# Reordering the prologue and the first steps of a 24-step recurrent scan on one Trainium2 core

## The chip, the cores and the metric

The kernel runs on one core of a Trainium2 chip. TensorE multiplies matrices, VectorE, ScalarE and GpSimd work elementwise, SyncE issues most transfers; the profile calls them PE, DVE, ACT, POOL and SP. The metric is device time in microseconds (us) of one execution, the median of several.

## The reference

For each of 4 x 8 heads a 40 x 40 state is carried over 768 time steps; the result goes through a gated feed-forward block.

```python
for t in range(S):                                   # S = 768
    y[:, :, t] = einsum('bhd,bhde->bhe', rt, state)
    Sa = einsum('bhde,bhe->bhd', state, at)
    state = state * wt[:, :, None, :] - einsum('bhd,bhe->bhde', Sa, bt)
    state = state + einsum('bhd,bhe->bhde', vt, kt)
x = y.transpose(0, 2, 1, 3).reshape(B, S, H * D)
h = maximum(x @ w_in, 0); u, v = halves of h         # 320 -> 1024
v_n = layernorm(v); v_s = einsum('ts,bsd->btd', w_spatial, v_n) + b_spatial
out = (u * v_s) @ w_out
```

## The kernel before, in words

The 768 time steps are cut into chunks of 64, and two batches (8 units of 2 heads) go together, so the first phase has 24 chunks, called steps 0 to 23. Inside a chunk the recurrence is a small triangular system; its solution lets the state jump 64 time steps at once. The second phase does the spatial product and the projection.

**What is made for a chunk before its step.** Its inputs arrive in a tile `ein` in two parts: W, the decay columns (528 columns), and O, the other operands (1536 columns). DVE runs two scans over W (`scan1`, L286, with a reciprocal L290; `scan2`, L295), giving running decay products `S` and `Et`. Then it multiplies: `at` (L312) from O and `Et`, `sl` (L318) from O and `S`. From `at` and `sl` PE makes the triangles (`lprime`, L331, 64 small products), and DVE masks them into `Lc` (`lblock`, L342). PE also makes `lka` (L392), `tok` (L444, transposes), `l21` (L461) and `h` (L422, from the tile `lin`), which ACT copies out of PSUM. ACT copies a column of `S` into the tiny tile `sc` (L304), which SP stores for a later step (`scr`, L306).

**The solve.** Four chunks' triangles are inverted together on DVE (`invert`, L350 to L367): a transpose, thirty pairs of products and additions, two more transposes into `XT0` (L365) and `X11` (L367). The first such solve stands alone in the prologue; later ones are spread through the steps. For each chunk PE and ACT then finish the inverse `xf`: `zt` (product L480, copies L489), copies of `XT0` (`b_xcopy`, L762) and `x21` (product L507, copies L516).

**A step.** `bp` (PE L538, reading the state `Mc`), its copies (ACT L548), `ff` (PE L556), copies `ffs` (ACT L564), `xx` (PE L574, needs `xf`), copies and masks (ACT L585, POOL L399), `mp` (PE L606), the new state `mn` and `Mc` (DVE L619, L620), and the output `y` (PE L630, DVE L643). There is one `bp` buffer per group of units, so the next step's `bp` waits for the DVE `y` instruction as well as for `Mc`.

**What sets the order.** In the first phase each engine runs its instructions strictly in the order in which they are written out; nothing reorders them. The prologue is straight code. From step 0 on a plan is used: `at(t, function, args)` enters a function at time t in units of steps, the plan is sorted by t, and the functions are called in that order. So a number such as 0.66 says how far through a step an item is issued, and an item that waits holds up everything behind it on its engine. While step s runs, the other work for chunk s+1 is issued (`b_...` functions), and the chunks' scans run some steps ahead: chunk 4 and 5's during step 0, 6 and 7's during step 1, 8 and 9's during step 2. The tiles `ein` of these are loaded in six pieces per chunk (`prep_piece`, L273, on SP) into two alternating buffers, a buffer being free once the chunk two earlier has made its `sl`.

Of the kernel before, what the change touches and what calls it, by code (L numbers as in the profile page):

```python
# [8 lines left out]
F32 = mybir.dt.float32  # L9
# [15 lines left out]
NU = NB * NP  # L25
GS = 4
# [185 lines left out]
def phase1(ctx, tc, early, late, vtok, win, xs, vns, uts, dscr):  # L212
# [48 lines left out]
    st = {}  # L261
# [58 lines left out]
            in1=sv[:, ns, 2:C + 2].unsqueeze(2).broadcast_to([P, k, 2, C]), op=ALU.mult,  # L320
        )

    def lprime(s):
        Et, at, sl = st["pre", s]
        pl = ps_k.tile([P, NU, HB], F32, name="bk")
        for n in range(NU):
            for blk in range(2):
                for par in range(2):
                    o = (1 - par) * 64 + blk * HB
                    cs = slice(blk * HB, (blk + 1) * HB)  # L330
                    nc.tensor.matmul(  # L331
                        pl[o:o + HB, n, :], lhsT=sl[PR[par], n, par, cs], rhs=at[PR[par], n, cs],
                        start=True, stop=True,
                    )
        st["pl", s] = pl

    def lblock(s):
        if s % GS == 0:
# [34 lines left out]
    def lin_load(s, par):  # L373
        nc.sync.dma_start(out=lin[s % 2][RR[par], :, 0:LATE], in_=late[par, s])
# [378 lines left out]
    def at(t, fn, *args):  # L753
        plan.append((t, len(plan), fn, args))
# [15 lines left out]
    for s in range(NS):  # L770
        at(s + 0.02, scn_load, s)
        for g in range(NB):
            at(s + 0.00 + 0.05 * g, c_bp, s, g)
            at(s + 0.04 + 0.05 * g, c_bp_out, s, g)
            at(s + 0.30 + 0.05 * g, c_ff, s, g)
            at(s + 0.34 + 0.05 * g, c_ff_out, s, g)
            at(s + 0.55 + 0.05 * g, c_xx, s, g)
            at(s + 0.60 + 0.05 * g, c_xx_out, s, g)
            at(s + 0.74 + 0.02 * g, c_mp, s, g)
            at(s + 0.755 + 0.02 * g, c_mp_out, s, g)  # L780
            at(s + 0.86 + 0.04 * g, c_y, s, g)
            at(s + 0.90 + 0.04 * g, c_y_out, s, g)
            at(s + 0.95 + 0.01 * g, y_store, s, g)
    for q in range(1, NS):
        b = q - 1
        for par in range(2):
            at(b + 0.11 + 0.02 * par, b_copy, q, par)
            at(b + 0.17 + 0.02 * par, b_lka_out, q, par)
            at(b + 0.72 + 0.02 * par, b_h_out, q, par)
            at(b + 0.40 + 0.03 * par, b_tok, q, par)  # L790
            at(b + 0.43 + 0.03 * par, b_tok_out, q, par)
        at(b + 0.115, b_lka, q)
        at(b + 0.52, b_l21, q)
        at(b + 0.54, b_l21_out, q)
        z = q % GS == 0
        at(b + (0.88 if z else 0.66), b_zt, q)
        at(b + (0.90 if z else 0.68), b_zt_out, q)
        at(b + 0.68, b_h, q)
        at(b + (0.975 if z else 0.50), b_xcopy, q, XC)
        at(b + (1.12 if z else 0.78), b_x21, q)  # L800
        at(b + (1.16 if z else 0.81), b_x21_out, q)
    for q in range(2, NS):
        for par in range(2):
            at(q - 2 + 0.20 + 0.14 * par, lin_load, q, par)
            at(q - 1 + 0.48 + 0.14 * par, vtok_load, q, par)

    LPO = 0.93
    PREP = {4: 0.03, 5: 0.45, 6: 1.03, 7: 1.45, 8: 2.03, 9: 2.45, 10: 3.03, 11: 3.45}
    for q in range(GS, NS):
        t = PREP.get(q, q - 8 + 0.01)  # L810
        at(t + 0.20, scan1, q)
        at(t + 0.28, scan2, q)
        at(t + 0.285, scr_store, q)
        at(t + 0.29, at_mul, q, AT_ENG)
        at(t + 0.30, sl_mul, q, SL_ENG)
        if q + 2 < NS:
            gap = 0.07 if q < 12 else 0.14
            for k in range(6):
                at(t + 0.40 + gap * k, prep_piece, q + 2, k)
        at(t + LPO, lprime, q)  # L820
        at(t + LPO + 0.05, lblock, q)
# [43 lines left out]
    with tc.manual_schedule():  # L865
# [11 lines left out]
            )  # L877
        pads(p, ein[2])
        pads(p, ein[3])
        for q in range(GS):  # L880
            for cols in (W, O):
                prep_load(q, 48 if q else 64, cols, q, qs)
        for par in range(2):
            lin_load(0, par)
            vtok_load(0, par)
# [10 lines left out]
        for q in range(2):  # L896
            for rows in RR:
# [1 line left out]
                nc.scalar.activation(  # L899
                    lin[q][rows, :, LATE:], diag.unsqueeze(1).broadcast_to([E, NU, E]), AF.Copy  # L900
                )
        for q in range(GS):
            scan1(q, q)
            scan2(q)
            at_mul(q, v)
            sl_mul(q, v)
            scr_store(q)
            lprime(q)
            if q:
                lblock(q - 1)  # L910
            if q == 0:
                b_copy(0, 0)
                b_copy(0, 1)
            if q == 1:
                b_lka(0)
                b_tok(0, 0)
                b_tok_out(0, 0)
            if q == 2:
                b_lka_out(0, 0)
                b_lka_out(0, 1)  # L920
                b_tok(0, 1)
                b_tok_out(0, 1)
                b_l21(0)
                b_l21_out(0)
        lblock(GS - 1)
        for par in range(2):
            lin_load(1, par)
            vtok_load(1, par)
        prep_load(4, 48)
        prep_load(5, 48)  # L930
        b_h(0)
        for _ in invert(0):
            pass
        b_h_out(0, 0)
# [71 lines left out]
```

## Time and profile before

| | us |
|---|---|
| median of 3 runs | 700.64 |
| lowest, highest | 698.61, 700.89 |
| the profiled execution, device time | 700.49 |
| its span in the profile | 698.8 |
| PE, DVE, ACT, POOL busy | 580.5, 445.9, 387.1, 297.7 |

The span runs from the first to the last instruction of the profile; the device time is 1.7 us longer. A timeline row gives start and busy time in us, then engine, source line, operation, output tile, input tiles, shapes and the number of instructions merged; the bracket at its end is the idle time of that engine just before and what ended it. A windows row gives for a stretch its length, the busy time of PE, PEld, DVE, ACT and POOL with instruction counts, then the granted PE clock, the busy share of the DMA engines and GB/s. A waits row gives who waited for whom, the us in total, the number of times and the longest.

### The profile page before, as it was taken

Reading aid. Unit: us, or ns where it says so; the run is one execution under the profiler, and the core shown is the slowest. Engines: PE = TensorE matmul, PEld = TensorE weight load, DVE = VectorE, ACT = ScalarE, POOL = GpSimd, SP = SyncE. Lnnn points to the kernel's source line nnn. Section 1 sums busy time; section 2 is a strip of 40 time slices with the busy share of each in tenths; the row PEclk is TensorE's granted clock in tenths of the full one; section 3 lists DMA queues with packets and bytes.
Section 4 is the critical chain, followed back from the end, with each engine's and each line's share of the span. In section 5 each row is a group of like instructions: output and inputs, shape, how many; then the busy total and the mean of one; then the engine's idle time right before and its main releaser. Section 6 shows DMA issues by size and latency. Waiting matters only on the chain. (4 is left out here: it accounts for less than half of the span.)

```text
span 698.8 us, 25621 instructions
## 1 busy us (share of the span) xinstructions
PE 580.5 (83%) x10784; PEld 528.8 (76%) x10784; DVE 445.9 (64%) x884; ACT 387.1 (55%) x856; POOL 297.7 (43%) x486
## 2 busy tenths in 40 slices
PE   1716885578777777999987999999999999999997
PEld 1615774477666667888876788788889989999997
DVE  7898779988999999968887366612128521332221
ACT  2305752356554666688867788898855442421112
POOL 5101332115434555364653434545448972462221
PEclk9965998678886986999999899999999999999999
DMA  9562877366454634766466355446345465550001
GB/s 184 97 115 50 141 146 138 74 145 135 102 131 107 142 83 122 142 152 153 118 174 197 89 146 149 123 131 166 97 139 170 132 177 162 164 180 28 29 30 57
DMA packets 106333, 87.68 MB, mean 125 GB/s; under 512 B 35497, under 2 KB 92073, under 8 KB 104297
## 3 DMA queue, kind: packets, MB, share of 16 engines
q1 hardware_dynamic: 105672, 84.31, 48.8%
q10 hardware_dynamic: 544, 1.72, 1.1%
q8 instruction: 85, 1.39, 0.9%
q14 instruction: 32, 0.25, 0.1%
HBM read 59.20 MB, written 20.50 MB: 114 GB/s over the span
## 5 line engine op out<-in xcount | busy, mean ns | idle before, releaser
L399 POOL TENSOR_SCALAR_AFFINE_SELECT Rt<-Rt 64x512 f32<-64x512 f32 (+1 forms) x144 | 86.4, 601 | 107.1 <-ACT Rt L585 73.6
L548 ACT ACTIVATE Rt<-bp 64x416 f32<-64x416 f32 x96 | 49.2, 512 | 73.3 <-PE bp L538 71.5
L538 PE MATMUL bp<-lin,Mc 40*64 40x104 f32 x768 | 52.2, 298 | 29.9 <-DVE y L643 29.3
L399 POOL TENSOR_SCALAR_AFFINE_SELECT At<-At 64x512 f32<-64x512 f32 x48 | 41.8, 871 | 77.2 <-ACT At L409 61.3
L356 DVE TENSOR_TENSOR itmp<-A 128x30 f32<-128x30 f32 (+9 forms) x180 | 72.0, 400 | 3.3
L538 PEld LDWEIGHTS bp<-lin,Mc 40*64 40x64 f32 x768 | 45.4, 164 | 33.2 <-DVE y L643 32.1
L173 PE MATMUL pg<-wsh,vh 128*128 128x384 f32 x192 | 65.2, 340 | 0.0
L174 PE MATMUL pg<-wsl,vh 128*128 128x384 f32 x192 | 65.2, 340 | 0.0
L175 PE MATMUL pg<-wsh,vl 128*128 128x384 f32 x192 | 65.1, 339 | 0.0
L360 DVE TENSOR_TENSOR A<-A,itmp 128x30 f32<-128x30 f32 (+9 forms) x180 | 59.0, 328 | 6.2
L177 DVE TENSOR_TENSOR g<-pg,bb 128x384 f32<-128x384 f32 x32 | 17.8, 556 | 65.0 <-PE pg L175 60.1
L54 POOL TENSOR_TENSOR gl<-g,gh 128x384 fp32r<-128x384 f32 x32 | 33.7, 1053 | 51.6 <-ACT gh L50 51.4
L585 ACT ACTIVATE Rt<-ch 64x416 f32<-64x416 f32 x96 | 49.2, 512 | 4.2 <-PE ch L574 1.8
L556 PE MATMUL ch<-Rt,At 128*64 128x104 f32 x768 | 46.6, 279 | 1.0 <-issue 1.0
L556 PEld LDWEIGHTS ch<-Rt,At 128*64 128x64 f32 x768 | 40.8, 154 | 5.4 <-issue 2.8
L50 ACT ACTIVATE gh<-g 128x384 fp32r<-128x384 f32 x32 | 16.6, 521 | 49.3 <-DVE g L178 49.1
L574 PE MATMUL ch<-ffs,xf 64*64 64x104 f32 x768 | 43.1, 266 | 0.0
L480 PE MATMUL bk<-XT,l 32*32 32x32 f32 x768 | 18.9, 201 | 28.4 <-DVE XT L365 26.4
L54 POOL TENSOR_TENSOR vl<-raw,vh 128x512 fp32r<-128x512 f32 x24 | 32.2, 1349 | 23.6 <-ACT vh L50 19.7
L480 PEld LDWEIGHTS bk<-XT,l 32*32 32x32 f32 x768 | 16.1, 116 | 32.8 <-issue 22.6
L708 DVE BATCH_NORM_STATS2 bs<-vr 128x6 f32<-128x512 f32 x24 | 16.6, 690 | 37.4 <-ACT vr L702 37.2
L444 PE MATMUL bk<-ident,sl 128*128 128x128 f32 x192 | 30.7, 301 | 11.7 <-ACT tk L450 7.0
(134 smaller groups left out, 1569.3 us busy)
## 6 DMA issues: line engine op xcount, KB each, us to landing
ein<-in_early SPq DMA_DIRECT2D x108, 129.0 KB
lin<-in_late SPq DMA_DIRECT2D x48, 160.0 KB
At<-at SPq DMA_DIRECT2D x48, 128.0 KB
uts<-ur SPq DMA_DIRECT2D x48, 128.0 KB
vns<-vr SPq DMA_DIRECT2D x24, 256.0 KB
raw<-vns SPq DMA_DIRECT2D x24, 256.0 KB
ut<-uts SPq DMA_DIRECT2D x24, 256.0 KB
Rt<-in_vtok SPq DMA_DIRECT2D x48, 80.0 KB
```

The lines of the kernel that those rows point to most:

```text
L54: eng.tensor_tensor(out=lo, in0=x, in1=hi.bitcast(F32), op=ALU.subtract)
L173: nc.tensor.matmul(pg, lhsT=vh[:, dc], rhs=w_h, start=(i == 0), stop=False)
L174: nc.tensor.matmul(pg, lhsT=vh[:, dc], rhs=w_l, start=False, stop=False)
L175: nc.tensor.matmul(pg, lhsT=vl[:, dc], rhs=w_h, start=False, stop=(i == NT - 1))
L356: nc.vector.tensor_tensor(out=tp, in0=A[:, k + 1:, k:k + 1].broadcast_to([P, m, k]), in1=A[:, k:k + 1, 0:k].broadcast_to([P, m, k]), op=AL ...
L360: nc.vector.tensor_tensor(out=A[:, k + 1:, 0:k], in0=A[:, k + 1:, 0:k], in1=tp, op=ALU.add)
L399: nc.gpsimd.affine_select(out=t, in_=t, pattern=[[0, k], [1, C]], base=0, channel_multiplier=-1, compare_op=ALU.is_gt, fill=0.0,)
L538: nc.tensor.matmul(bp[PR[par], q, :], lhsT=Mc[RR[par], n, :], rhs=li[RR[par], n, C:], start=(q == 0), stop=False, skip_group_check=True,)
L548: nc.scalar.activation(Rt[par][PR[par], gp, :], st["bp", g][PR[par]], AF.Copy)
L556: nc.tensor.matmul(ff[PR[1 - par], q, :], lhsT=At[par][:, n, :], rhs=Rt[par][:, n, :], start=True, stop=True,)
L574: nc.tensor.matmul(xx[ev, q, :], lhsT=xf[ev, n, :], rhs=ffs[ev, q, :], start=True, stop=True,)
L585: nc.scalar.activation(Rt[par][PR[par], gp], xx[PR[1 - par]], AF.Copy, scale=-1.0)
```

## The change

The functions of the plan stay; no arithmetic is removed or added, except that `sl` of the first four chunks is made in two halves of units. What moves:

- the prologue loads the W parts of chunks 0 and 1 first, then their O parts;
- DVE runs the scans of chunk 1 before `at` and `sl` of chunk 0;
- for chunks 0 to 3, `sl` and `lprime` alternate by halves of the units, and `lka`, `tok`, `l21` of chunk 0, with their copies, come after all triangles instead of among them;
- the `sc` copies of chunks 0 to 3, the `At` transfers and the load of chunk 4 are placed after the last `lblock`;
- in step 0 the `sc` copy of chunk 4 goes from 0.315 to 0.68, the `sl` of chunk 5 from 0.75 to 0.83, and the products of chunk 1 get times of their own (table `FIRST`);
- the pieces of `ein` of chunks 6 to 9 are issued 0.03 apart instead of 0.07.

```diff
-    def lprime(s):
+    def lprime(s, units=range(NU)):
         Et, at, sl = st["pre", s]
-        pl = ps_k.tile([P, NU, HB], F32, name="bk")
-        for n in range(NU):
+        if units[0] == 0:
+            st["pl", s] = ps_k.tile([P, NU, HB], F32, name="bk")
+        pl = st["pl", s]
+        for n in units:
...
+    REG = dict(copy=0.11, lka=0.115, lka_out=0.17, tok=0.40, tok_out=0.43, l21=0.52, l21_out=0.54,
+               zt=0.66, zt_out=0.68, h=0.68, h_out=0.72, x=0.50, x21=0.78, x21_out=0.81, dt=0.03)
+    LEAD = dict(REG, zt=0.88, zt_out=0.90, x=0.975, x21=1.12, x21_out=1.16)
+    FIRST = dict(REG, tok=0.37, tok_out=0.375, l21=0.45, l21_out=0.452, zt=0.47, zt_out=0.50, x=0.70,
+                 h=0.80, h_out=0.81, x21=0.65, x21_out=0.71)
...
+    SCR, SLM = {4: 0.68}, {5: 0.83}
...
-        at(t + 0.285, scr_store, q)
+        at(SCR.get(q, t + 0.285), scr_store, q)
         at(t + 0.29, at_mul, q, AT_ENG)
-        at(t + 0.30, sl_mul, q, SL_ENG)
+        at(SLM.get(q, t + 0.30), sl_mul, q, SL_ENG)
         if q + 2 < NS:
-            gap = 0.07 if q < 12 else 0.14
+            gap = 0.03 if q < 8 else 0.07 if q < 12 else 0.14
...
-        for q in range(GS):
-            for cols in (W, O):
-                prep_load(q, 48 if q else 64, cols, q, qs)
+        for q, cols in ((0, W), (1, W), (0, O), (1, O), (2, W), (2, O), (3, W), (3, O)):
+            prep_load(q, 48 if q else 64, cols, q, qs)
...
-        for q in range(GS):
+        for q in range(2):
             scan1(q, q)
             scan2(q)
+        for q in range(GS):
+            if q > 1:
+                scan1(q, q)
+                scan2(q)
             at_mul(q, v)
-            sl_mul(q, v)
-            scr_store(q)
-            lprime(q)
+            for h in range(2):
+                sl_mul(q, v, grp(h)[0])
+                lprime(q, grp(h)[1])
             if q:
                 lblock(q - 1)
-            if q == 0:
-                b_copy(0, 0)
-                b_copy(0, 1)
-            if q == 1:
-                b_lka(0)
-                b_tok(0, 0)
-                b_tok_out(0, 0)
-            if q == 2:
-                b_lka_out(0, 0)
-                b_lka_out(0, 1)
-                b_tok(0, 1)
-                b_tok_out(0, 1)
-                b_l21(0)
-                b_l21_out(0)
         lblock(GS - 1)
+        for par in range(2):
+            b_copy(0, par)
+        prep_load(4, 48)
+        for q in range(GS):
+            scr_store(q)
+        b_lka(0)
+        for par in range(2):
+            b_lka_out(0, par)
+            b_tok(0, par)
+            b_tok_out(0, par)
+        b_l21(0)
+        b_l21_out(0)
+        b_h(0)
         for par in range(2):
+            b_h_out(0, par)
             lin_load(1, par)
             vtok_load(1, par)
-        prep_load(4, 48)
         prep_load(5, 48)
-        b_h(0)
         for _ in invert(0):
             pass
-        b_h_out(0, 0)
-        b_h_out(0, 1)
...
         at(0.42, b_zt, 0)
-        at(0.43, b_zt_out, 0)
-        at(0.44, b_xcopy, 0, act_copy)
+        at(0.43, b_xcopy, 0, act_copy)
+        at(0.44, b_zt_out, 0)
         at(0.455, b_x21, 0)
         at(0.46, b_x21_out, 0)
```

Three places in the order show it. In the changed file most line numbers are one higher.

On PE in the prologue, up to the first `bp`, before (`bk` is whatever PSUM tile the small products go to; `at,sl` 32x32 are the triangles, 64x64 is `lka`, `ident` is `tok`, `sl,at` is `l21`, `lin` is `h`):

```order
L331 MATMUL bk<-at,sl 32x32 x64
L392 MATMUL bk<-at,sl 64x64 x16
L444 MATMUL bk<-ident,sl 128x128 x4
L331 MATMUL bk<-at,sl 32x32 x32
L444 MATMUL bk<-ident,sl 128x128 x4
L461 MATMUL bk<-sl,at 32x32 x16
L331 MATMUL bk<-at,sl 32x32 x32
L422 MATMUL bk<-lin_136 64x64 x16
```

And now:

```order
L333 MATMUL bk<-at,sl 32x32 x128
L393 MATMUL bk<-at,sl 64x64 x16
L445 MATMUL bk<-ident,sl 128x128 x8
L462 MATMUL bk<-sl,at 32x32 x16
L423 MATMUL bk<-lin_136 64x64 x16
```

All four chunks' triangles now stand together, ahead of `lka`, `tok` and `l21`.

On ACT in step 0, from the first chunk's last copies before the solve's results to the copies of `xx`, before (`XT` and `xf` are the solve's result and the finished inverse, `l` is `l21`):

```order
L304 ACTIVATE sc<-S 128x8
L564 ACTIVATE ffs<-ch 128x416 x2
L450 ACTIVATE tk<-bk 128x320
L489 ACTIVATE zt<-bk 32x256 x2
L762 ACTIVATE xf_130<-XT_557 128x8x32
L762 ACTIVATE xf_130<-XT_557 32x8x32 x2
L450 ACTIVATE tk<-bk 128x320
L516 ACTIVATE xf_130<-bk 32x8x32 x2
L762 ACTIVATE xf_131<-XT_557 128x8x32
L762 ACTIVATE xf_131<-XT_557 32x8x32 x2
L470 ACTIVATE l_745<-bk 32x256 x2
L585 ACTIVATE Rt_132<-ch 64x416
```

And now:

```order
L565 ACTIVATE ffs<-ch 128x416
L451 ACTIVATE tk<-bk 128x320
L565 ACTIVATE ffs<-ch 128x416
L451 ACTIVATE tk<-bk 128x320
L763 ACTIVATE xf_130<-XT_565 128x8x32
L763 ACTIVATE xf_130<-XT_565 32x8x32 x2
L490 ACTIVATE zt<-bk 32x256 x2
L471 ACTIVATE l_722<-bk 32x256 x2
L517 ACTIVATE xf_130<-bk 32x8x32 x2
L490 ACTIVATE zt<-bk 32x256 x2
L586 ACTIVATE Rt_132<-ch 64x416
```

The `sc` copy is gone from the head of the row (it stands after the copies of `xx`), and both `tk` copies stand ahead of everything that needs `XT`.

On SP, from the loads for step 2 in step 0 to the second `scn` load, before (`ein` 16x2064 are the pieces):

```order
L374 DMA lin_136<-in_late 40x8x128
L306 DMA scr<-sc 40x8 x2
L374 DMA lin_136<-in_late 40x8x128
L273 DMA ein_120<-in_early 16x2064 x5
L306 DMA scr<-sc 40x8 x2
L273 DMA ein_120<-in_early 16x2064
L273 DMA ein_121<-in_early 16x2064 x3
L527 DMA scn<-scr 64x320 x2
```

And now:

```order
L375 DMA lin_136<-in_late 40x8x128 x2
L273 DMA ein_120<-in_early 16x2064 x6
L306 DMA scr<-sc 40x8 x4
L273 DMA ein_121<-in_early 16x2064 x6
L528 DMA scn<-scr 64x320 x2
```

The six pieces of chunk 6 stand ahead of the stores of `sc`, and all six of chunk 7 ahead of the `scn` load.

More of the change, by code (lines that the diff above doesn't have):

```diff
@@ L334, in lprime @@
                     )
-        st["pl", s] = pl
     def lblock(s):
@@ L783, in phase1 @@
             at(s + 0.95 + 0.01 * g, y_store, s, g)
+    REG = dict(copy=0.11, lka=0.115, lka_out=0.17, tok=0.40, tok_out=0.43, l21=0.52, l21_out=0.54,
[3 more added lines that the diff above has]
+                 h=0.80, h_out=0.81, x21=0.65, x21_out=0.71)
     for q in range(1, NS):
-        b = q - 1
+        T = {k: q - 1 + t for k, t in (FIRST if q == 1 else REG if q % GS else LEAD).items()}
+        dt = T["dt"] - q + 1
         for par in range(2):
[L787 to L801, printed above, removed]
+            at(T["copy"] + 0.02 * par, b_copy, q, par)
+            at(T["lka_out"] + 0.02 * par, b_lka_out, q, par)
+            at(T["h_out"] + 0.02 * par, b_h_out, q, par)
+            at(T["tok"] + dt * par, b_tok, q, par)
+            at(T["tok_out"] + dt * par, b_tok_out, q, par)
+        at(T["lka"], b_lka, q)
+        at(T["l21"], b_l21, q)
+        at(T["l21_out"], b_l21_out, q)
+        at(T["zt"], b_zt, q)
+        at(T["zt_out"], b_zt_out, q)
+        at(T["h"], b_h, q)
+        at(T["x"], b_xcopy, q, XC)
+        at(T["x21"], b_x21, q)
+        at(T["x21_out"], b_x21_out, q)
     for q in range(2, NS):
```

## The prediction

> **What bounds the kernel now.** I read the windows view first, over the stretches of step 0 (56:72), steps 1, 2 and 3, steps 4 to 11 and the rest of the first phase:
>
> ```profile
> 56.00:72.00 16.00, 12.52 (x358) 11.13 (x360) 13.11 (x17) 11.09 (x28) 3.77 (x6) 0.65 0.40 71
> 72.00:90.00 18.00, 13.80 (x464) 12.18 (x465) 12.96 (x19) 11.50 (x27) 7.14 (x8) 1.00 0.86 143
> 90.00:116.00 26.00, 15.97 (x470) 14.18 (x468) 21.13 (x44) 11.56 (x27) 6.28 (x8) 0.85 0.76 140
> 116.00:145.00 29.00, 16.31 (x416) 14.74 (x414) 27.71 (x58) 11.01 (x25) 4.51 (x8) 0.68 0.39 87
> 145.00:300.00 155.00, 124.94 (x3209) 112.85 (x3207) 142.98 (x268) 96.77 (x217) 67.85 (x79) 0.83 0.57 125
> 300.00:534.00 234.00, 219.75 (x4469) 191.54 (x4466) 131.26 (x302) 181.97 (x402) 119.39 (x236) 0.98 0.53 144
> ```
>
> From 116 to 145 DVE is busy 27.71 of 29.00 us, and from 145 to 300 142.98 of 155: DVE's queue sets the pace there. From 300 to 534 it is PE, 219.75 of 234. Both queues run in a fixed order, so whatever makes DVE reach the work at 116 earlier moves all that follows by the same amount, unless a slower clock takes it back. Before 116 DVE is not full. Its waits between 60 and 120 us:
>
> ```profile
> DVE S L286 <- DMA ein<-in_early: 5.8, 3, 2.8
> DVE mn L619 <- PE ch L606: 2.4, 1, 2.4
> DVE S L286 <- DMA scr<-sc: 1.6, 1, 1.6
> ```
>
> That is 9.8 us, of which 7.4 (the first and third row) is the scans of chunks 6 to 9 waiting for their pieces, the last put down to `scr` by the profile. Then the prologue, in the page's line of GB/s in 40 slices and in the timeline:
>
> ```profile
> GB/s 184 97 115 50 141 146 138 74 145 135 102 131 107 142 83 122 142 152 153 118 174 197 89 146 149 123 131 166 97 139 170 132 177 162 164 180 28 29 30 57
> ...
> 4.95 1.26 DVE L286 TENSOR_TENSOR_SCAN S<-ein,ends 128x528 f32<-128x528 f32 x1 [1.27 <-DMA ein<-in_early]
> 9.35 0.69 DVE L312 TENSOR_TENSOR at<-ein,Et 128x512 f32<-128x512 f32 x1 [1.55 <-DMA ein<-in_early]
> 9.96 1.22 DVE L318 TENSOR_TENSOR sl<-ein,S 128x1024 f32<-128x1024 f32 x1
> 24.71 1.66 DVE L318 TENSOR_TENSOR sl<-ein,S 128x1024 f32<-128x1024 f32 x1
> 27.61 1.06 PE L331 MATMUL bk<-at,sl 64*32 64x32 f32 x58
> 28.73 0.42 DVE L342 TENSOR_TENSOR Lc<-bk,maskl 128x256 f32<-128x256 f32 x1 [2.02 <-PE bk L331]
> 29.18 1.95 DVE L350 STREAM_TRANSPOSE A<-Lc 128x1024 f32<-128x1024 f32 x1
> ```
>
> DVE idles 1.55 us for chunk 0's O part and 2.02 us for chunk 3's triangles, which PE makes only after `tok` and `l21`; one `sl` takes 1.66 instead of 1.22. The solve starts at 29.18.
>
> **Part 1: the prologue.** To be won: 1.55 + 2.02 + 0.44 = 4.0 us. To be paid: `sl` in two halves, each like the 512-column `at` at 0.69, so 2 x 0.69 - 1.22 = 0.16 for a chunk, 0.6 for four; and PE's last half of the triangles, half of 1.06, of which the 0.42 of the preceding `Lc` hides most, with a handoff 0.3. Net 3.0 if all loads come in time. Two scans and a reciprocal fill 4.95 to 7.80 (9.35 less the wait); chunk 1's fill another 2.85, to 10.65. O of chunk 0 now follows chunk 1's W, which is 96 rows of 2112 bytes, 0.20 MB, 1.1 us at the 184 GB/s of the first slice: it comes at about 10.45, just in time. Chunk 1's O, 0.59 MB, comes 3.2 us behind it, at 13.65, and is wanted at 12.55: up to 1.1 lost, none if the queues run faster than their mean with the start in it. The later parts come 1 us or more before they are wanted, reckoned in the same way. I take the middle, 2.5, between the bounds 1.9 and 4.0. The `lka`, `tok`, `l21`, `h` and `bp` work that is pushed back lies beside the solve, at whose end PE idles 18.46 us and ACT 23.35 (brackets below); it would cost only what outlasts that.
>
> **Part 2: step 0.** The solve's end and what follows it:
>
> ```profile
> 53.90 1.90 DVE L365 STREAM_TRANSPOSE XT<-A 128x1024 f32<-128x1024 f32 x1
> 55.94 1.06 PE L480 MATMUL bk<-XT,l 32*32 32x32 f32 x32 [18.46 <-DVE XT L365]
> 57.40 1.33 DVE L286 TENSOR_TENSOR_SCAN S<-ein,ends 128x528 f32<-128x528 f32 x1
> 58.76 0.21 ACT L304 ACTIVATE sc<-S 128x8 f32<-128x8 f32 x1 [23.35 <-DVE S L286]
> 60.00 0.74 ACT L489 ACTIVATE zt<-bk 32x256 f32<-32x256 f32 x2
> 60.77 1.15 ACT L762 ACTIVATE xf<-XT 128x256 f32<-128x256 f32 x3
> 61.22 1.06 PE L507 MATMUL bk<-zt,X 32*32 32x32 f32 x32
> 62.39 0.77 ACT L516 ACTIVATE xf<-bk 32x256 f32<-32x256 f32 x2
> 63.42 3.04 PE L574 MATMUL ch<-ffs,xf 64*64 64x104 f32 x32
> 64.86 0.69 DVE L312 TENSOR_TENSOR at<-ein,Et 128x512 f32<-128x512 f32 x1
> 68.42 0.81 PE L606 MATMUL ch<-tk,Rt 128*40 128x40 f32 x32
> 69.07 0.33 DVE L619 TENSOR_TENSOR mn<-ch,Mc 104x160 f32<-104x160 f32 x1 [2.38 <-PE ch L606]
> 70.92 0.85 DVE L643 TENSOR_TENSOR y<-bp,Et 104x256 f32<-104x256 f32 x2
> 71.93 1.38 PE L538 MATMUL bp<-lin,Mc 40*64 40x104 f32 x26
> ```
>
> ACT stood 23.35 us at the tiny `sc` copy, whose scan comes only after both last transposes, with the copies of `ffs`, `tk` and `zt` queued behind it. So `zt`'s product was done at 57.00 and copied at 60.00, and `xx` (L574) started 63.42 - 55.80 = 7.6 us after `XT0`. Now: product 1.06 (the `XT0` copies, 1.15, beside it), copies 0.74, product 1.06, copies 0.77, and four handoffs of about 0.1: 4.0 us. So `xx` starts 3.6 us sooner after the solve, 6.1 in all, at 57.3. Chunk 1's `zt` product and `l21` copies fit into PE's and ACT's waits there.
>
> DVE then decides. It does `at` of chunk 5 (end 65.55) 2.5 us earlier, at 63.05; `mp` is ready, 5.0 us after `xx` at about 62.3. So `mn` starts at 63.05 with no wait. From `mn` to the end of `y` it took 71.77 - 69.07 = 2.7; the moved `sl` adds 1.22: 67.0, and `bp` of step 1 starts at 67.1 instead of 71.93, 4.8 us earlier. The other bound: PE ran `xx` at half clock (3.04; 0.65 granted in 56:72). If it does the rest of the step at half clock, the 3.5 us from `mp` to `bp` (68.42 to 71.93), mostly PE's, become 7, `bp` comes near 69, and the gain is 3.0. I take 4.8, since PE is busy without a break from 53.4 on now and was at full clock in 72:90, when it had again been busy for some us.
>
> [...]
>
> **Part 3: steps 1 and 2.** Rows of SP, PE and DVE:
>
> ```profile
> 62.15 2.17 SPq L273 DMA_DIRECT2D ein<-in_early  x5
> 69.39 0.66 SPq L306 DMA_DIRECT2D scr<-sc  x2
> 70.09 1.70 SPq L273 DMA_DIRECT2D ein<-in_early  x4
> 87.34 0.64 PE L630 MATMUL bp<-Rt,tk 128*40 128x64 f32 x14 [0.65 <-POOL Rt L399]
> 89.68 1.26 PEld L538 LDWEIGHTS bp<-lin,Mc 40*64 40x64 f32 x28
> 92.58 1.26 DVE L286 TENSOR_TENSOR_SCAN S<-ein,ends 128x528 f32<-128x528 f32 x1 [2.34 <-DMA ein<-in_early]
> 103.61 1.26 DVE L286 TENSOR_TENSOR_SCAN S<-ein,ends 128x528 f32<-128x528 f32 x1 [1.56 <-DMA scr<-sc]
> 103.89 0.81 PE L606 MATMUL ch<-tk,Rt 128*40 128x40 f32 x32
> 109.77 0.32 DVE L619 TENSOR_TENSOR mn<-ch,Mc 104x160 f32<-104x160 f32 x1
> ```
>
> Chunk 6's sixth piece stood behind the `scr` store of chunk 5, whose `sc` copy came late: five pieces went out from 62.15, the sixth at 70.09. Now all six go together, and chunk 7's as soon as its buffer is free. Step 1 itself is mostly PE, ACT and POOL one after another, so DVE's waits there are worth little: PE's products for `y` ended at 87.98 and `bp` started at 89.68, because DVE was still at `Mc`; of that 1.7 the `y` instruction and a handoff need 0.6, so 1.1 is won, and `bp` of step 2 comes 5.9 earlier.
>
> In step 2 DVE sets the pace: `mp` was done at 104.70, `mn` came at 109.77. The scan of chunk 8 loses its wait of 2.34, that of chunk 9 its 1.56, if the pieces come sooner by that much: 5.9 + 2.34 + 1.56 = 9.8, and `mn` at 100.0 is still after `mp` at 98.8. If no wait goes, 5.9, or less. The pieces' buffer is freed earlier by the same shift, and the last piece of chunk 8 no longer stands behind a store; but DMA is at 0.86 in 72:90, and a chunk's pieces wait for the `vtok` load as before. I leave a third of the 3.9 as still waited for, 1.3, and take 8.5.
>
> **Sum.** 2.5 + 2.3 (4.8 at step 1's `bp`) + 1.1 + 2.6 = 8.5 us. The profiled execution took 700.49 (span 698.8), 0.15 under the median of 700.64: 692.0 us. Its own bounds: 690.7 with no wait left; 693.8 with half clock in step 0.
>
> **Rivals.**
> - *The pieces bind again.* DMA at 0.86 and 0.76 speaks for it; that the pieces were held by SP's order and not by bandwidth (70.09) against. The 3.9 of step 2 and part of step 1's 1.1 stay: gain 4.8, 695.7 us.
> - *Taken back later.* From 145 to 300 PE is busy 124.94 of 155 at a granted 0.83. Were the clock to fall to 0.78 as the work packs closer, PE's 125 us would grow by 125 x (0.83 / 0.78 - 1) = 8 us and the gain be gone: 700 us. Also here: a wait on a copy that was moved in the prologue which I don't see.
> - *Slower.* PE stays at half clock through step 1. Its 13.80 us of work there become 27.6, 9.6 more than the step's 18.0. With 3.0 won before it, `bp` of step 2 is 6.6 late; DVE's two waits, 3.9, vanish in that; 2.7 us slower, 703.2. It decides if half clock lasts beyond some 84 us. For it: 0.65 and 0.70 stand over long stretches. Against: the 1.00 of 72:90. [...]
>
> **How the numbers follow.** Forecast 0.55, pieces bind 0.25, taken back 0.13, slower 0.07. A measurement here tells about 0.3%, 2.1 us, from no change. The first two are faster, and 0.02 of the third; of the slower case 0.01 stays within: faster 0.82, same 0.12, slower 0.06. The range runs from 688.0 (12.5 won: nearly all the 4.0 + 9.8 of waits) to 697.5 (beyond the pieces' rival by 1.8).
>
> **What would show it.** The solve's transpose near 26.7 instead of 29.18; `xx` 4 us after `XT0` ends, near 57.3; the first `bp` of step 1 near 67.1; the scans of chunks 6 to 9 with waits of about 1.3 in sum instead of 7.4; `mn` of step 2 near 101.3; then the same shift in every later row, at 0.83 of the clock. Wrong if DVE waits in the prologue for chunk 1's O, if `y` of step 0 waits for PE at half clock, or if the shift at 145 is gone at 300.

## The result, and the profile after

The changed kernel takes **694.61 us** (median of 4 runs, 693.37 to 695.17) against 700.76 for the kernel before, measured beside it (4 runs, 698.61 to 701.86): ratio **0.9913**, 95% interval 0.9886 to 0.9941. The same kernel measured again later, in 8 runs: 693.78 against 701.45, ratio 0.9894 (0.9856 to 0.9931). By these medians it won 6 to 8 us of the 8.5 forecast. Medians are of all runs; ratios and intervals leave out the runs that are over 1.5% above the fastest of their kernel, of the changed kernel none. The profiled execution took 695.17 us, 5.3 less than the profiled one before (700.49).

Where it was won is read in time order. First the prologue, in the timeline of the changed kernel:

```profile
10.51 1.33 DVE L318 TENSOR_TENSOR sl<-ein,S 128x512 f32<-128x512 f32 x2
12.11 0.69 DVE L312 TENSOR_TENSOR at<-ein,Et 128x512 f32<-128x512 f32 x1 [0.27 <-DMA ein<-in_early]
24.82 0.42 DVE L343 TENSOR_TENSOR Lc<-bk,maskl 128x256 f32<-128x256 f32 x1 [0.44 <-PE bk L333]
25.28 1.94 DVE L351 STREAM_TRANSPOSE A<-Lc 128x1024 f32<-128x1024 f32 x1
49.56 1.91 DVE L366 STREAM_TRANSPOSE XT<-A 128x1024 f32<-128x1024 f32 x1
```

The wait for chunk 1's O part is 0.27, the wait for the last triangles 0.44 instead of 2.02, two halves of `sl` take 1.33 together, and the solve starts at 25.28 instead of 29.18. Its `XT0` ends at 51.47, 4.3 earlier. Then step 0, same view:

```profile
51.56 1.15 ACT L763 ACTIVATE xf<-XT 128x256 f32<-128x256 f32 x3 [9.12 <-DVE XT L366]
55.59 3.04 PE L575 MATMUL ch<-ffs,xf 64*64 64x104 f32 x32
59.55 1.19 PE L607 MATMUL ch<-tk,Rt 128*40 128x40 f32 x32
61.17 0.31 DVE L620 TENSOR_TENSOR mn<-ch,Mc 104x160 f32<-104x160 f32 x1
63.74 0.76 DVE L644 TENSOR_TENSOR y<-bp,Et 104x256 f32<-104x256 f32 x2
64.22 1.38 PE L539 MATMUL bp<-lin,Mc 40*64 40x104 f32 x26 [0.59 <-DVE y L644]
```

ACT now waits for `XT0` and not for `sc`; `xx` starts 4.1 us after `XT0` ends; the row of `mn` has no bracket, so it did not wait; `y` of step 0 ends at 64.50 instead of 71.77, 7.3 earlier. From there on the lead does not grow. The windows view, for the last two stretches that the prediction shows:

```profile
145.00:300.00 155.00, 122.02 (x3178) 110.57 (x3168) 144.43 (x272) 99.17 (x223) 73.89 (x86) 0.87 0.54 124
300.00:534.00 234.00, 221.27 (x4370) 192.46 (x4371) 127.79 (x298) 178.22 (x390) 119.52 (x241) 0.97 0.52 143
```

DVE still fills 145:300 (144.43 of 155) and PE 300:534 (221.27 of 234). The end of `y`, step by step, from the last `y` row of each:

| end of `y` of step | before | after | the same kernel again |
|---|---|---|---|
| 0 | 71.77 | 64.50 | 65.23 |
| 1 | 89.68 | 82.83 | 81.12 |
| 2 | 115.57 | 109.34 | 108.25 |
| steps 1 and 2 together | 43.8 | 44.8 | 43.0 |

So steps 1 and 2, in which 3.7 us were to be won, gave -1.0 in one profile and +0.8 in another. What stood there is in the view of waits, 60 to 120 us:

```profile
DVE Lc L343 <- PE bk L333: 6.3, 3, 2.8
DVE mn L620 <- PE ch L607: 3.0, 1, 3.0
DVE S L286 <- DMA ein<-in_early: 1.2, 1, 1.2
```

In this profile the scans' waits fell from 7.4 to 1.2, as forecast (1.3); in the second one, below, they are 5.4. In their place DVE waits 6.3 us for PE's triangles and 3.0 for `mp`: 10.5 in all. Before, the same stretch had, beside the three rows that the prediction shows (9.8 us), a fourth, which it left out:

```profile
DVE Lc L342 <- PE bk L331: 1.4, 2, 1.1
```

That makes 11.2. The waits were hardly fewer; they had changed their cause. Why PE was late is in part in the same trace: PE itself stood still for 5.8 us in these two steps (rows below, "PE's stalls"), and part of the time it ran at half clock. The granted clock of 60:90 is 0.84 here (third number from the row's end), and 1.00 in the second profile:

```profile
60.00:90.00 30.00, 23.57 (x680) 21.32 (x678) 21.01 (x33) 17.26 (x40) 9.51 (x13) 0.84 0.83 141
```

### The profile page after: what moved, and what is told of

It is laid out like the page before. It is cut to its first block, busy times and chain, and to the rows that moved or that the text cites. A ratio compares the mean times of both kernels' runs of the same rounds, so it can differ in the third digit from the quotient of the medians.

```text
span 693.4 us, 25634 instructions
## 1 busy us (share of the span) xinstructions
PE 582.2 (84%) x10784; PEld 530.5 (77%) x10784; DVE 442.9 (64%) x888; ACT 388.2 (56%) x856; POOL 302.8 (44%) x486
## 3 DMA queue, kind: packets, MB, share of 16 engines
q8 instruction: 85, 1.39, 0.9%
## 5 line engine op out<-in xcount | busy, mean ns | idle before, releaser
L400 POOL TENSOR_SCALAR_AFFINE_SELECT Rt<-Rt 64x512 f32<-64x512 f32 (+1 forms) x144 | 89.4, 623 | 91.8 <-ACT Rt L586 71.5
L357 DVE TENSOR_TENSOR itmp<-A 128x30 f32<-128x30 f32 (+9 forms) x180 | 69.5, 386 | 3.2
L557 PE MATMUL ch<-Rt,At 128*64 128x104 f32 x768 | 49.2, 291 | 0.0
L557 PEld LDWEIGHTS ch<-Rt,At 128*64 128x64 f32 x768 | 44.0, 164 | 4.6 <-issue 1.3
L333 PE MATMUL bk<-at,sl 64*32 64x32 f32 x1536 | 21.6, 206 | 27.8 <-DVE sl L318 19.9
L333 PEld LDWEIGHTS bk<-at,sl 64*32 64x32 f32 x1536 | 18.2, 117 | 30.8 <-issue 16.3
L393 PE MATMUL bk<-at,sl 64*64 64x64 f32 x768 | 37.3, 265 | 2.0 <-issue 2.0
```

The lines of the kernel that those rows point to most:

```text
L357: nc.vector.tensor_tensor(out=tp, in0=A[:, k + 1:, k:k + 1].broadcast_to([P, m, k]), in1=A[:, k:k + 1, 0:k].broadcast_to([P, m, k]), op=AL ...
L400: nc.gpsimd.affine_select(out=t, in_=t, pattern=[[0, k], [1, C]], base=0, channel_multiplier=-1, compare_op=ALU.is_gt, fill=0.0,)
L557: nc.tensor.matmul(ff[PR[1 - par], q, :], lhsT=At[par][:, n, :], rhs=Rt[par][:, n, :], start=True, stop=True,)
```

## The experiments

Kernels that were measured side by side share their runs of the kernel before, whose single runs lie mostly between 698 and 706 us; a difference of 1.5 us between two variants is therefore not told by these intervals. All ratios are to the kernel before. The early pieces, the 32 added products and the two single edits were not measured beside the changed kernel; with it they are compared best by their ratios. The experiments answer four questions: do the parts add up, does the spacing do anything, what holds steps 1 and 2, and which single edit carries each part.

### The parts alone

New prologue, old plan:

```diff
-        T = {k: q - 1 + t for k, t in (FIRST if q == 1 else REG if q % GS else LEAD).items()}
+        T = {k: q - 1 + t for k, t in (REG if q % GS else LEAD).items()}
-    SCR, SLM = {4: 0.68}, {5: 0.83}
+    SCR, SLM = {}, {}
-            gap = 0.03 if q < 8 else 0.07 if q < 12 else 0.14
+            gap = 0.07 if q < 12 else 0.14
```

(and `b_zt_out` ahead of `b_xcopy` again in step 0)

> The new prologue alone; the plan of step 0 and the spacing of the pieces are those of before. In the two profiles the solve's transpose XT0 ends 4.3 us earlier (55.80 to 51.47). Theory A (the prologue's shift is carried whole to the end): 4.3 us faster, about 696.4. Rival (a moved start only moves the wait at the tiny sc copy and the waits for pieces): 2 us or less, 698.5 or more.

Measured 698.81, ratio 0.9952 (0.9923 to 0.9981): 1.3 to 5.4 us won. That does not decide between the two: the interval holds the theory's 4.3 us, and the median is on the rival's side (698.5 or more). The timeline has the solve 3.5 earlier; `y` of step 0 ends 3.4 earlier, at 68.34, and that of step 2 3.6 earlier, but that of step 23 only 1.7 (532.10 against 533.77):

```profile
25.70 1.94 DVE L351 STREAM_TRANSPOSE A<-Lc 128x1024 f32<-128x1024 f32 x1
```

Old prologue, new plan of step 0 (the tables `FIRST`, `SCR` and `SLM` of the change, of which the cut shows a part; `gap` of 0.07):

```diff
+    SCR, SLM = {4: 0.68}, {5: 0.83}
-        at(t + 0.285, scr_store, q)
+        at(SCR.get(q, t + 0.285), scr_store, q)
...
-        at(0.43, b_zt_out, 0)
-        at(0.44, b_xcopy, 0, act_copy)
+        at(0.43, b_xcopy, 0, act_copy)
+        at(0.44, b_zt_out, 0)
```

> The new plan of step 0 alone (table FIRST, the sc copy of chunk 4 at 0.68, the sl of chunk 5 at 0.83, XT0 copies ahead of zt's); prologue and spacing as before. From the end of XT0 to the end of y of step 0 it took 15.98 us before and 13.0 after. Theory A: some 3 us won in step 0, of which PE's stalls and waits in steps 1 and 2 take back about 1: 1.5 to 3 us faster, 698 to 699. Rival (the forecast's part 3): 2.3 from step 0 and more behind it: 3.4 or more, 697.3 or less.

Measured 698.27 (697.36 over the nine runs of the ratio), ratio 0.9935 (0.9894 to 0.9975), 1.8 to 7.4 us won. The ranges of theory and rival (1.5 to 3, and 3.4 or more) both meet it. The two parts give 0.48% and 0.65%, together 1.1%; the whole change gives 0.9 to 1.1%. Within their wide intervals they add up, with no sign of a gain by the spacing. The spacing alone:

```diff
-            gap = 0.07 if q < 12 else 0.14
+            gap = 0.03 if q < 8 else 0.07 if q < 12 else 0.14
```

> Only the pieces of chunks 6 to 9 are issued 0.03 apart instead of 0.07, all else as before. Forecast (the waits of the scans, 3.9 us in step 2, are worth 2.6): 698.0 or less. Rival (PE, ACT and POOL in a row set steps 1 and 2, so the scans' waits are worth next to nothing): 700.0 to 701.0.

Measured 701.87, ratio 1.0005 (0.9974 to 1.0036): no gain, and the forecast's 2.6 us (a ratio of 0.9963) lies outside the interval. DVE's waits between 60 and 116 us:

```profile
DVE mn L619 <- PE ch L606: 4.3, 2, 3.5
DVE Lc L342 <- PE bk L331: 2.8, 2, 2.2
DVE S L286 <- DMA ein<-in_early: 1.6, 1, 1.6
DVE y L643 <- PE bp L630: 1.6, 3, 0.8
```

Only the order of loads on SP was touched, and the scans' 7.4 us of waiting fell to 1.6. DVE's waits are still 10.3 in sum, after 11.2 before: what it waits for PE grew from 3.8 (`mn` 2.4, `Lc` 1.4) to 8.7. Not all of that answers the earlier pieces. Of the 8.7, 4.7 lie in step 0, before its `y` ends at 73.07, where PE ran at half clock throughout (0.50 in 56:72, against 0.65 in the prediction's row). In steps 1 and 2 alone the waits for PE grew from 1.4 to 4.0, all waits fell from 8.8 to 5.6, and the two steps took 40.7 us instead of 43.8. So in this one profile the earlier pieces go with 3.1 us less in steps 1 and 2; a slower step 0 and a loss behind step 2 (1.8 ahead at its end, 0.6 behind at the end of step 23) took that back. In the twelve times nothing of it is left.

The whole change with the old spacing, measured twice:

```diff
-            gap = 0.03 if q < 8 else 0.07 if q < 12 else 0.14
+            gap = 0.07 if q < 12 else 0.14
```

> The changed kernel with the old spacing 0.07 of the pieces. Forecast's part 3: the waits for pieces come back, 697 or so. Rival (they are worth nothing in the changed kernel, where DVE waits for PE's triangles and mp instead): 694.0 to 695.5, and DVE waits for ein where it now waits for PE.

> The changed kernel with the old spacing 0.07 once more. Theory A (the new spacing is worth nothing; e4's lead was spread): the same as the changed kernel beside it within 1.5 us. Theory B (the new spacing does harm: the pieces issued in a burst hold up the fetches of PE's instructions, and PE stalls in steps 1 and 2, 5.8 us of it in the changed kernel's profile and 0.4 in e4's): 1.5 to 3 us faster than the changed kernel beside it.

The first gave 693.19 (0.9875, 0.9827 to 0.9922), the second 694.97 (0.9929, 0.9901 to 0.9957), the change itself beside the second 693.78 (0.9894, 0.9856 to 0.9931). No difference is told in either direction, and so no harm by the burst either. Here the scans wait again and PE's triangles do not hold DVE (the two largest rows and that of the triangles, first of the two, 55 to 116 us):

```profile
DVE S L286 <- DMA lin<-in_late: 5.8, 1, 5.8
DVE S L286 <- DMA ein<-in_early: 2.7, 2, 2.4
DVE Lc L343 <- PE bk L333: 0.3, 1, 0.3
```

The first of these rows is the scan of chunk 7, for whose wait the profile names `lin`; the last packet of the chunk's pieces ends at 77.81, and the scan begins at 80.24.

### What holds steps 1 and 2

The changed kernel again, unaltered:

> The changed kernel once more, beside the next three on the same chip. All theories: 0.987 to 0.994 of before, as at first. It gives the spread against which the next three are read.

693.78, as given above. Its profile shows other waits than the first profile of the same program (the largest rows, 55 to 116 us):

```profile
DVE S L286 <- DMA ein<-in_early: 3.7, 1, 3.7
DVE S L286 <- DMA scr<-sc: 1.7, 1, 1.7
DVE Lc L343 <- PE bk L333: 1.5, 1, 1.5
```

and in its timeline, for chunk 8:

```profile
77.78 3.12 SPq L273 DMA_DIRECT2D ein<-in_early  x4
86.67 1.32 DVE L286 TENSOR_TENSOR_SCAN S<-ein,ends 128x528 f32<-128x528 f32 x1 [3.67 <-DMA ein<-in_early]
```

The last piece is issued by 80.9, its last packet ends at 85.5 and the scan begins at 86.67. To see what these transfers cost in all, they were left out: the pieces of chunks 8 and 9 are not loaded, so two chunks are computed from other data.

```diff
-        if q + 2 < NS:
+        if q + 2 < NS and q not in (6, 7):
```

> The changed kernel without the loads of chunks 8 and 9 (their scans take what lies in the buffers; two chunks' results are another computation's): 1.6 MB less to move in steps 1 and 2. Forecast's part 3 (DVE waits for pieces set step 2): no more won than what DVE still waits for pieces there, under 1 us. Theory B (the pieces hold up PE's instruction fetches): PE's stalls in steps 1 and 2 fall from 5.8 to under 2 us and the kernel is 2 to 4 us faster than the changed one beside it. Rival (the stalls hang on how dense PE's instructions are): stalls of 4 us or more stay, within 1 us of the changed one.

688.81, ratio 0.9827 (0.9781 to 0.9872), 5.0 us under the changed kernel measured beside it. The expectation from part 3 of the prediction, under 1 us, is missed. Steps 1 and 2 take 38.3 us (65.34 to 103.66) instead of 43.0. DVE's waits are nearly gone:

```profile
DVE S L286 <- DMA scr<-sc: 2.0, 1, 2.0
DVE mn L620 <- PE ch L607: 0.6, 1, 0.6
DVE Lc L343 <- PE bk L333: 0.3, 1, 0.3
```

The first row is the scan of chunk 6, whose pieces are still loaded: their last packet ends at 66.00 and the scan begins at 67.65, about as long after it as in the other profiles. So it most likely waited for the pieces and not for the store that is named. PE's stalls in the two steps are 0.7 us, where the two profiles of the changed kernel have 5.8 and 1.4.

The busy share of the DMA engines between 60 and 90 us is 0.56 here and 0.80 there (fourth and third number from a windows row's end are the clock and the share; first this kernel, then the changed one):

```profile
60.00:90.00 30.00, 25.25 (x843) 22.27 (x839) 26.36 (x39) 21.46 (x52) 13.84 (x16) 1.00 0.56 115
```

```profile
60.00:90.00 30.00, 22.93 (x776) 20.05 (x770) 21.53 (x32) 19.44 (x46) 13.96 (x15) 1.00 0.80 129
```

So about 5 us of the time, and 4.7 of steps 1 and 2 in the two profiles, hang on these twelve transfers. Can they be had by loading earlier? The pieces of chunks 8 and 9 were put right behind the `sl` that frees their buffer, and the `sc` copies and stores of chunks 6 and 7 behind them:

```diff
-    SCR, SLM = {4: 0.68}, {5: 0.83}
+    SCR, SLM = {4: 0.68, 6: 1.45, 7: 1.90}, {5: 0.83}
-                at(t + 0.40 + gap * k, prep_piece, q + 2, k)
+                at(t + 0.301 + 0.001 * k if q in (6, 7) else t + 0.40 + gap * k, prep_piece, q + 2, k)
```

> The changed kernel with the pieces of chunks 8 and 9 put on SP right behind the sl that frees their buffer (times t + 0.301 to 0.306 instead of 0.40 to 0.55), ahead of vtok, and the sc copies and stores of chunks 6 and 7 behind them. In the changed kernel's second profile sl of chunk 6 ended at 72.6, its six successors' pieces were issued from 76.1 to 80.9 and the scan came at 86.7; without these loads 5 us were won. Theory A (SP's order holds the pieces back): 2.5 to 4.7 us faster than the changed kernel, 0.983 to 0.987 of before, and the scans of chunks 8 and 9 wait under 1 us. Rival (the transfers are held by DMA, busy 1.06 in 78:84): within 1 us of the changed kernel, 0.988 to 0.993, the scans wait as before.

693.18 (691.51 over the eight runs of the ratio), ratio 0.9856 (0.9820 to 0.9892). The ratio lies in the theory's range and its interval reaches into the rival's. In the timeline all six pieces of chunk 8 leave from 72.05 on and its scan has no wait, as the theory had it:

```profile
72.05 3.37 SPq L273 DMA_DIRECT2D ein<-in_early  x6
84.38 0.52 PE L333 MATMUL bk<-at,sl 64*32 64x32 f32 x36 [2.09 <-issue]
84.94 0.42 DVE L343 TENSOR_TENSOR Lc<-bk,maskl 128x256 f32<-128x256 f32 x1 [2.20 <-PE bk L333]
85.28 1.25 DVE L286 TENSOR_TENSOR_SCAN S<-ein,ends 128x528 f32<-128x528 f32 x1
```

But DVE now waits 2.20 for `Lc`, because PE stood 2.09 us in the middle of 64 triangles whose inputs were there. Steps 1 and 2 take 43.2 us (64.49 to 107.66), no less than in the changed kernel again (43.0). So in this profile the 5 us are not won, and whether this version beats the changed kernel at all is not told by the intervals.

The traces show what decides. They are cut here at the ends of `y` of steps 0 and 2, and DVE's waits of over 0.15 us between these are added up (us, one execution each):

| kernel | steps 1 and 2 | waits of scans | waits for PE | the rest |
|---|---|---|---|---|
| before | 43.8 | 7.4 | 1.4 | 35.0 |
| changed | 44.8 | 1.2 | 9.4 | 34.2 |
| changed, again | 43.0 | 5.4 | 2.5 | 35.1 |
| spacing alone | 40.7 | 1.6 | 4.0 | 35.1 |
| changed, old spacing | 43.9 | 9.1 | 0.3 | 34.6 |
| the same again | 43.3 | 7.6 | 0.3 | 35.5 |
| changed, without the pieces | 38.3 | 2.0 | 0.9 | 35.5 |
| changed, early pieces | 43.2 | 1.7 | 6.4 | 35.1 |

The rest, in which DVE mostly works, is nearly the same everywhere. What differs is the sum of its waits, and where the scans wait less, DVE mostly waits more for PE. DVE does set the pace of these steps, as the prediction says; a wait taken from a scan is won only if it does not come back at the triangles or at `mp`.

### PE's stalls

The rows "issue" on PE were the second suspect: time in which PE waits for nothing that the profile shows. In the changed kernel's two profiles and in that of the early pieces they fall on the same products:

```profile
67.43 1.54 PE L393 MATMUL bk<-at,sl 64*64 64x64 f32 x24 [1.56 <-issue]
84.85 0.75 PE L333 MATMUL bk<-at,sl 64*32 64x32 f32 x36 [2.48 <-issue]
```

(first profile) and, in the second,

```profile
67.03 0.92 PE L393 MATMUL bk<-at,sl 64*64 64x64 f32 x24 [0.43 <-issue]
82.01 0.52 PE L333 MATMUL bk<-at,sl 64*32 64x32 f32 x36 [0.99 <-issue]
```

Always ahead of the last 24 of `lka` and the last 36 of the triangles; only the length changes, 0.42 to 1.56 and 0.99 to 2.48. In the trace's list of DMA packets each stall of the first profile's steps 1 and 2 ends shortly after a packet of the instruction queue has ended (read packet by packet, us):

```
instruction packet     stall of PE ends    after the packet's end
64.28 to 65.90         67.42               1.52
71.17 to 72.61         74.03               1.42
75.95 to 77.55         79.28               1.73
81.69 to 83.15         84.85               1.70
```

The idea was that these products are the first of a new block of instructions, one block to a packet. A packet of this queue has 16384 bytes; the page counts 85 of them and, on PE, 10784 products and as many weight loads, 254 instructions to a packet. To move the blocks, 64 small products without use were put among the prologue's triangles:

```diff
+            if q == 0:
+                for _ in range(64):
+                    nc.tensor.matmul(pv[0:HB, 0:HB], lhsT=ident[0:HB, 0:HB], rhs=ident[0:HB, 0:HB],
+                                     start=True, stop=True)
```

> The changed kernel with 64 idle products of 32 x 32 put on PE behind the first chunk's triangles: PE's later instructions lie half of a 256-instruction fetch block further on. Theory: PE's stalls come at the end of a fetch (1.4 to 1.7 us after it in both profiles), so they move to other products and their sum in steps 1 and 2 (5.8 us) changes, and the time with it by 1 to 3 us, up or down. Rival (the stalls hang on the transfers alone): the same stalls at the same products, the time within 1 us of the changed kernel's.

697.86, ratio 0.9950 (0.9922 to 0.9978), 4.1 over the changed kernel measured beside it, more than either had expected. The stalls stayed at the same products, and the timeline says why nothing was told by that: the 64 products as written became 128 with 128 weight loads (10912 of each on its page, after 10784), and these 256 instructions are a whole block: its page has 86 packets, one more.

```profile
13.32 7.03 PE L922 MATMUL pv<-ident 32*32 32x32 f32 x128
52.45 1.91 DVE L366 STREAM_TRANSPOSE XT<-A 128x1024 f32<-128x1024 f32 x1
```

They held up the triangles behind them, and `XT0` came at 52.45 instead of 50.31 in the changed kernel's second profile. The time is 4.1 longer for a prologue 2.1 later, and that is not a shift carried through: by the ends of `y` in the two profiles the lag is 2.1 at step 0, 1.0 at step 2 (109.22 against 108.25) and 5.3 at step 23 (532.55 against 527.28). What was lost behind step 2 stays unexplained. Then 32 of them, 64 products, placed beside the solve, where PE has nothing to do:

```diff
         prep_load(5, 48)
+        for _ in range(32):
+            nc.tensor.matmul(pv[0:HB, 0:HB], lhsT=ident[0:HB, 0:HB], rhs=ident[0:HB, 0:HB],
+                             start=True, stop=True)
         for _ in invert(0):
```

> The changed kernel with 32 idle products of 32 x 32 (128 PE instructions, half a fetch block) put where PE idles beside the solve; e7's 64 were a whole block, moved no boundary, and cost PE 7 us where DVE waited. Theory (PE's stalls come at fetch boundaries): the stalls of steps 1 and 2 leave L393 and L333 and come at other products; the time within 2 us of the changed kernel either way. Rival (they hang on those products or on the transfers beside them): the stalls stay at L393 and L333.

691.17, ratio 0.9866 (0.9823 to 0.9909). The stalls moved:

```profile
63.97 0.56 PE L333 MATMUL bk<-at,sl 64*32 64x32 f32 x40
65.57 0.39 PE L333 MATMUL bk<-at,sl 64*32 64x32 f32 x24 [1.05 <-issue]
82.23 1.47 PE L539 MATMUL bp<-lin,Mc 40*64 40x104 f32 x28
85.45 0.31 PE L539 MATMUL bp<-lin,Mc 40*64 40x104 f32 x2 [1.75 <-issue]
```

The count fits exactly. Before, the first stall stood behind 8 products of `lka`; these follow 32 of `bp` and 64 triangles. Sixty-four products earlier is 8 + 32 + 24: behind the first 40 triangles, where the row has it. The second stood behind 28 of 64 triangles, with a `bp` behind them; a grid of 128 moved by 64 has its next line 36 + 28 products on: behind 28 of `bp`, where the row has it. So PE's stalls lie on a grid of 128 products with their loads, that is 256 instructions. The other rows "issue" fit: counted through the profile before, its eleven stalls lie 126 to 128 recorded products apart, or whole multiples of that. The time did not clearly change with where they lie: the median is 2.6 below that of the changed kernel, a little beyond the 2 us expected, but the intervals overlap.

### The single edits

The old order of loads in the changed kernel:

```diff
-        for q, cols in ((0, W), (1, W), (0, O), (1, O), (2, W), (2, O), (3, W), (3, O)):
+        for q, cols in ((0, W), (0, O), (1, W), (1, O), (2, W), (2, O), (3, W), (3, O)):
```

> The changed kernel with the prologue's loads in the old order (W and O of chunk 0, then of chunk 1). Theory (the scans of chunk 1 filling the wait for chunk 0's O is worth 1.55 us): the first scan of chunk 1 now waits for its W behind that O, the solve starts about 1.5 us later and the kernel is 1.5 us slower than the changed one. Rival (the loads' order only moves the wait): no difference, under 0.5 us.

695.27, ratio 0.9910 (0.9883 to 0.9936). The theory's 1.5 us over the changed kernel and the rival's nothing both lie inside. In the trace the second scan waits, and the solve starts 2.5 later than in the first profile after, 2.1 later than in the second (25.71):

```profile
10.14 1.26 DVE L286 TENSOR_TENSOR_SCAN S<-ein,ends 128x528 f32<-128x528 f32 x1 [2.14 <-DMA ein<-in_early]
27.80 1.95 DVE L351 STREAM_TRANSPOSE A<-Lc 128x1024 f32<-128x1024 f32 x1
```

In time that is 0.7 to 1.5 us over the two medians of the changed kernel, and its ratio lies between their two; the intervals do not tell it from nothing. The trace shows the 2 us in the prologue, and at the end of step 2 it has hardly any of them: `y` ends at 109.21 there, against 109.34 and 108.25. That speaks for the rival.

The tiny `sc` copy of chunk 4 back at its old place:

```diff
-    SCR, SLM = {4: 0.68}, {5: 0.83}
+    SCR, SLM = {}, {5: 0.83}
```

> The changed kernel with the sc copy of chunk 4 back at its old place, ahead of ffs, tk and zt on ACT; the rest of step 0's new plan stays. Theory (the tiny copy was what held the solve's copies): zt's copies wait for the scan of chunk 4 again, xx starts some 3 us later after XT0 than the 4.1 of the changed kernel, and all that step 0's plan gave is lost: 2.5 to 3.5 us slower than the changed kernel. Rival (the order of the products gave it, or DVE sets step 0 anyhow): 1 us or less.

698.15, ratio 0.9957 (0.9931 to 0.9984), 3.5 to 4.4 us over the changed kernel. Its timeline:

```profile
53.91 0.21 ACT L304 ACTIVATE sc<-S 128x8 f32<-128x8 f32 x1 [17.65 <-DVE S L286]
59.19 2.85 PE L575 MATMUL ch<-ffs,xf 64*64 64x104 f32 x32
63.25 0.33 DVE L620 TENSOR_TENSOR mn<-ch,Mc 104x160 f32<-104x160 f32 x1 [2.55 <-ACT Rt L586]
```

An instruction of 0.21 us holds ACT for 17.65; `xx` starts 8.2 us after `XT0` (ended at 51.01) instead of 4.1, and `mn` waits again. From the end of `XT0` to the end of step 0's `y` it takes 15.6 us, where the changed kernel takes 13.0 and the kernel before 16.0. So this one number, 0.68 for 0.315, carries 2.5 of the 3.0 us of the second part.

## Why the prediction was right, and where it was not

The time (692.0 forecast, range 688.0 to 697.5) and the sign held. That the number came so near is in part luck: parts 1 and 2 gave more than was forecast, and part 3 nothing.

- **Part 1, the prologue: right, sized too low.** 2.5 was taken between 1.9 and 4.0; measured at the solve's start 3.9, by the rows 29.18 and 25.28 (3.5 in the second profile, at 25.71). 2.5 is the middle of 1.9 and 3.0, not of the bounds that are named. The 1.1 feared for chunk 1's O part was 0.27 (in the second profile nothing, but chunk 0's O part was waited for 0.87). The halves cost 1.33 - 1.22 = 0.1 a chunk, where 0.16 was reckoned. And the first scan began at 4.48 (4.35) instead of 4.95, for which the sum had no term.
- **Part 2, step 0: right.** `xx` 4.0 us after `XT0`: 4.1. `mn` without a wait: so. `bp` of step 1 at 64.22, 7.7 earlier instead of 4.8: 1.8 of the difference is the earlier `XT0` (4.3 against 2.5), and `mn` to `bp` took 3.05 instead of 4.0. The clock: `xx` still ran at half speed (3.04 for 32 products, 1.64 in step 1, at 75.08), and so, for the most part, did `mp` (1.19, against 0.81 in the prediction's row at 68.42); the products behind it no longer did. The granted clock is 0.53 in 46:60 and 0.84 in 60:70 (windows of the profile after), and within these it rose at 60.5 (0.50 in 56:60.4, 1.00 in 60.6:64):

```profile
46.00:60.00 14.00, 8.39 (x206) 7.85 (x208) 13.38 (x23) 6.43 (x17) 2.07 (x2) 0.53 0.12 25
60.00:70.00 10.00, 7.85 (x232) 7.22 (x229) 8.57 (x15) 6.07 (x14) 4.69 (x6) 0.84 0.86 129
```

  The 4.8 took PE to be at full clock from `mp` on, since it would have been busy without a break by then. How much work brings the clock up, no run shows: in the profile after, PE worked without a wait from 51.6 on, and the clock rose 8.9 us later, in `mp`; in the second profile it rose 6.4 us later (52.4 to 58.8), ahead of `mp` at 59.72, and in that of the spacing alone some 15 us later (59.3 to 74.2). The gain of step 0 in the profile after did not hang on it, since DVE came to `mn` only when `mp` was done; to that extent the term was right by luck.
- **Part 3, steps 1 and 2: wrong.** The step that failed: "The scan of chunk 8 loses its wait of 2.34, that of chunk 9 its 1.56 ... 5.9 + 2.34 + 1.56 = 9.8", of which 2.6 was kept, and the 1.1 of step 1. Measured in place of 3.7: -1.0 and +0.8. That the scans would lose their waits held in one profile of the changed kernel (1.2 left) and not in the other (5.4); with nothing but the spacing changed 1.6 were left. That a wait lost by a scan is time won did not hold: the text asked only whether `mn` would still come after `mp`. DVE also needs PE's triangles for `Lc` in each step, and `mp`, and PE was no further along: in the first profile DVE waited 9.4 us for PE in these steps, where it had been 1.4, in the second 2.5. The row of 1.4 for `Lc`, left out of the prediction, was the sign of it. The term of 1.1 in step 1 was not tested by itself.
- **The carry: right for the changed kernel.** 6.2 us of lead at the end of step 2 are 4.9 at the end of step 23 (`y` ends at 533.77 and 528.85) and 5.3 at the end, and 7.3 are 6.5 in the second profile; the granted clock of 145:300 is 0.87, not lower. The rival "taken back later" did not come here; nor did "slower", whose half clock through step 1 had to last to 84 us, though half clock did come back for a part of step 1 (the 0.84 of 60:90). It is no law: in the other profiles the lead changed between these two points by anything from 5.1 us lost (the 64 products) to 3.2 gained (the 32).
- **The rival "the pieces bind again"** put 695.7, nearer to 694.61 than the forecast. Its statement is half right: the transfers still cost 5 us (688.81 without them), but not only as waits of the scans. In one profile of the changed kernel the scans wait 5.4 us; in the other they hardly wait, and PE stands still and is late. That the transfers are what makes PE late there is argued, not shown.

The ledger of the profiled pair: 7.3 at `y` of step 0 (forecast 4.8), -1.0 in steps 1 and 2 (forecast 3.7), -1.3 up to step 23, and 0.4 more won in the second phase: 5.3, against a sum of 8.5.

Open: how the 5 us of the transfers divide between late pieces and a late PE, which in one execution trade against each other; how much of PE's lateness is its stalls and how much its half clock, since the first profile has more of both; whether DMA load is what lengthens the stalls (in steps 1 and 2 they are 0.7 us without the twelve transfers, but also 0.4 and nothing with all of them at the old spacing, and 5.8 and 1.4 in two executions of one program); and whether the early pieces are worth anything.

## What to carry to other kernels

A tiny copy that waits for late data, on an engine that works in order, costs what stands behind it (here 0.21 us that held ACT for 17.65, and 3.5 to 4.4 us of the kernel's time): look for the longest bracket on the copying engine and read the next rows, not the copy. A wait that is removed is worth something only if every other supplier of the waiting engine is early too; write down, for the stretch, all that the engine waits for, and when each would be ready without the first. Time won ahead of a long chain of full queues was carried almost whole to the end in both profiles of the changed kernel (4.9 us of 6.2, and 6.5 of 7.3), but not in every variant; a shift seen early in a trace is not yet time.

## What the runs showed of the hardware that was not expected

**PE stalls on instruction blocks.** Waits "issue" on PE add up over a whole execution to 11.1 us before, 15.7 after and 7.5 in the second profile of the same changed kernel, single ones up to 2.8. The page of the profile has the packets that belong to it, 85 of 16.4 KB (1.39 MB), the same number in all three:

```profile
q8 instruction: 85, 1.39, 0.9%
```

The kernel with 256 more PE instructions (128 products and their loads) has 86 of them, one more. A packet takes 1.4 to 1.6 us in the four cases above, and PE goes on 1.4 to 1.7 after its end; over all thirty stalls of the three profiles it is 1.3 to 2.1. The products here are short: 64 triangles take 0.76 us where nothing stops them (timeline after),

```profile
71.33 0.76 PE L333 MATMUL bk<-at,sl 64*32 64x32 f32 x64
```

so that a block of 128 products can be used up in about 1.5 us (an estimate from this row), as long as a packet takes. Most blocks pass without a stall: 7 to 12 in 85. The counts give the size of a block: 21568 instructions on PE (10784 products and as many loads) in 85 packets, 21824 in 86, and 21696 in 85 with the 32 added products. At 256 to a packet these come to just 85, 86 and 85, and the grid of 128 products and their loads agrees. The 2.48 us of the row at 84.85 stand on such a boundary.

**One product written, two made.** Each of the added float32 products was two products and two weight loads on PE: 64 written are 128 (x128 in the row at 13.32; 128 more products and 128 more loads on the page), 32 written are 64 (10848 of each, after 10784).

**Two executions of one program wait in different places.** With times 0.3% apart (695.17 and 692.79), the changed kernel waited 6.3 us for triangles in one and 3.7 us for a piece in the other. A single profile's list of waits near a balance of two engines is one sample.
